# Joint 64-feature products for two pairs of weight blocks in the fourth batch's first MLP half

## The chip, the cores and the metric

The kernel runs on one core of one Trainium2 chip. Its engines work side by side, each on its own queue of instructions: TensorE (PE, matmuls, with PEld for the loads of its weights), VectorE (DVE), ScalarE (ACT), GpSimd (POOL) and SyncE (SP), which issues the transfers. They wait for each other through semaphores. Matmuls write to PSUM, which has eight banks of 512 float32 numbers in each of 128 partitions; the vector engines read it from there. The metric is the device time of one execution, in microseconds (us).

## The reference, cut to what matters

Two blocks follow each other, for 4 batches of 768 tokens. First an mLSTM cell with 8 heads of 40 features: a recurrence over the tokens with gates. Its output, 320 features per token, goes into a Fourier mixing block with an MLP:

```
X = np.real(np.fft.fft(np.fft.fft(x, axis=1), axis=2))
u = x + X
un = (u - mean(u)) / np.sqrt(var(u) + 1e-06)
out = u + np.maximum(un @ w_ch1, 0.0) @ w_ch2      # w_ch1: 320 x 1280, w_ch2: 1280 x 320
```

The change is in `un @ w_ch1`, the MLP's first half, of the last batch. All is in float32, and a float32 matmul runs in two passes, which the profile counts as two.

## The kernel before, in words

The program is written out by hand: `at(slot, phase, function, ...)` puts a call into a plan, and `run` carries the plan out in the order of slot and phase. So the order of each engine's queue follows from slots and phases alone; within a slot, phases run from EVAC (0) over FILL (1) and MAIN (2) to FILL_PE (3). Semaphores are put in by the language: an instruction waits for the earlier ones on other engines that use the same tile. Batches overlap: while one batch is in its MLP, the next is in its recurrence and its Fourier mix. The fourth batch has nothing behind it, so its MLP runs alone at the end.

The eight PSUM banks: four are handed out by number, as tiles `pm`, `po`, `px` and so on, by `bank(name, shape, n)`. The other four are two tiles of two banks each, `scores` and `heads` (named `ps` and `ph` in the profile), which serve the recurrence. When the fourth batch's MLP starts, the recurrence has ended and they are idle.

The first half for batches 1 to 3 (counted from 0): the 1280 hidden features are ten blocks of 128, taken as five pairs, numbered 0 to 4. The 768 tokens are two groups of 384, `gr` 0 and 1. The 320 input features are two parts of 128 (`ch` 0 and 1 of the weights, `mlp_u(gr, 0)` and `mlp_u(gr, 2)`) and one of 64 (`mlp_u(gr, 1)`). For each pair, the 2 x 2 block product over the two 128-feature parts is done with seven products in place of eight (Winograd's form), with sums of weights S2, S3, S4 and of inputs T2, T3, T4. The products go into four banks, which the code calls p1, p2, p5 and p3. What p1 holds is copied out by ScalarE in between, and the rest is added by VectorE. The 64 features that are left are multiplied in `rest_products` (line 1129): four matmuls on quarters of the array, 64 x 64 each, that run side by side, for each group of tokens.

`mlp_block(b, i, step)` (line 1207) issues pair i. Its steps, in order on TensorE:

- `begin(i)`: first product, into p1; ScalarE copies p1 to the hidden block `h11`, that is `hidden(0, 2i)`; its buffer is called h00 (h10, h11 and h01 are the buffers of `h12`, `h22` and `h21`). For pair 0 it runs at step 0, for the others at step 3 of the pair before.
- step 0: the product into p2.
- step 1: the S2 product on top of p1, which ScalarE copies to `h12`; the product into p5, which VectorE adds to `h12`.
- step 2: the S4 product into p3; the S3 product on top of p1, which ScalarE copies to `h22`.
- step 2.5: the 64-feature products, first of group 1 into p3 and p5, then of group 0 into p2 and p1. Then VectorE's three adds: p3 to `h12`, p5 to `h22`, p2 to `h11`.
- step 3: `begin(i + 1)`; then the T4 product on top of p1, from which ScalarE takes `h21` with a relu.

The three hidden blocks that VectorE finished get their relu in place by ScalarE in the next pair's slots (`mlp_relu_in_place`, planned at line 1391). An even pair takes its banks 3, 2, 1, 0 for p1, p2, p5, p3, an odd pair 0, 1, 2, 3. So `begin(i + 1)` writes into the bank that held p3 of pair i and waits for VectorE's add of it.

The second half (`mlp_out_pair`, line 1333) needs sums over hidden blocks, `hidden_sums` (line 1324), S1 to S4 in the profile. Those of the first pair of token tiles are planned at lines 1406 to 1409: for weight-block pairs 0 to 2 during the last slots of the first half, for pairs 3 and 4 at its end. `banks` in the lines quoted is, inside `mlp_block`, the list of bank numbers:

```
banks = list(range(4) if i % 2 else range(3, -1, -1))
```

Of the kernel before, what the change touches and what calls it, by code (L numbers as in the profile page):

```python
# [14 lines left out]
AF = mybir.ActivationFunctionType  # L15
# [3 lines left out]
B, H, S, D = 4, 8, 768, 40  # L19
L = 128  # L20
# [8 lines left out]
NFF = DFF // L  # L29
TAIL = DM - 2 * L  # L30
TG = NT // 2
# [26 lines left out]
def kernel(  # L58
# [15 lines left out]
    nc = tc.nc  # L74

    def pool(name, bufs, **kw):
        return ctx.enter_context(tc.tile_pool(name=name, bufs=bufs, **kw))
# [16 lines left out]
    def bank(name, shape, n=None):  # L94

        return ps_m.tile(shape, FP, name=name, tag=f"pm{next(turn) if n is None else n}")
# [31 lines left out]
    def at(slot, phase, fn, *args):  # L128
        plan.setdefault((slot, phase), []).append((fn, args))
# [7 lines left out]
    EVAC, FILL, MAIN, FILL_PE = range(4)  # L137
# [303 lines left out]
    class Piece:  # L441
# [15 lines left out]
        def take(self):  # L457
            if self.float:
                return
            n = self.src.shape[1]  # L460
            words = self.raw.bitcast(U32).rearrange("p (m two) -> p m two", two=2)
            self.lo, self.hi = words[:, :, 0], words[:, :, 1]
            self.e = cp.tile([L, n], U32, name="e", tag="e", bufs=1)
            self.m = cp.tile([L, n], U32, name="m", tag="m", bufs=1)
            nc.vector.tensor_scalar(out=self.e, in0=self.hi, scalar1=20, scalar2=0x7FF, op0=OP.logical_shift_right,  # L465
                                    op1=OP.bitwise_and)
            nc.vector.tensor_scalar(out=self.m, in0=self.hi, scalar1=0xFFFFF, scalar2=0x100000, op0=OP.bitwise_and,
                                    op1=OP.bitwise_or)
# [32 lines left out]
    def w1_block(ch, f):  # L501
        return w1_sb[:, f // 2, (2 * ch + f % 2) * L:(2 * ch + f % 2 + 1) * L]

    def w1_rest(n):
        return w1_sb[:, n, 4 * L:]
# [80 lines left out]
    def product(out, w, x, start):  # L586
        nc.tensor.matmul(out, w, x, start=start, stop=True, skip_group_check=True)  # L587
# [69 lines left out]
    banks = {}  # L657
# [10 lines left out]
    def half(n):  # L668
        return slice(n * LH, (n + 1) * LH)
# [459 lines left out]
    def rest_products(banks, n, u, start):  # L1129


        for cols in range(2):
            for i in range(2):
                nc.tensor.matmul(banks[i][half(cols)], w1_rest(n)[half(i), half(cols)], u[half(i)], start=start,  # L1134
                                 stop=not start, skip_group_check=True)
# [29 lines left out]
    def hidden(gr, f):  # L1165
        return hid[gr, f % 2][:, f // 2 * TG * L:(f // 2 + 1) * TG * L]
# [8 lines left out]
    def block(t, n):  # L1175
        return t[:, n * L:(n + 1) * L]
# [20 lines left out]
    def mlp_u(gr, ch):  # L1197
        return uT_bufs[gr][:, ch].rearrange("p c t -> p (c t)")
# [8 lines left out]
    def mlp_block(b, i, step):  # L1207

        k = mixes[b]
        f = 2 * i
        T2, T3, T4 = w1x["T"]
        A = {(r, ch): w1_block(ch, f + r) for r in range(2) for ch in range(2)}

        def product(bank, w, u, start=False):
            nc.tensor.matmul(bank, w, u, start=start, stop=True, skip_group_check=True)  # L1217

        def tails(gr, banks):
            rest_products(banks, i, mlp_u(gr, 1), False)  # L1220

        def add(h, bank):
            nc.vector.tensor_tensor(out=h, in0=h, in1=bank, op=OP.add)  # L1223

        banks = list(range(4) if i % 2 else range(3, -1, -1))

        def begin(i):


            k.p1 = bank("pm", [L, TG * L], 0 if i % 2 else 3)  # L1230
            product(k.p1, w1_block(0, 2 * i), mlp_u(0, 0), True)
            nc.scalar.copy(out=hidden(0, 2 * i), in_=k.p1)

        (h11, h21), (h12, h22) = ([hidden(gr, f + r) for r in range(2)] for gr in range(2))
        if step == 0:
            if i == 0:
                begin(0)
            k.pm = [k.p1, bank("pm", [L, TG * L], banks[1])]
            product(k.pm[1], A[0, 1], mlp_u(0, 2), True)
        elif step == 1:  # L1240
            k.pm.append(bank("pm", [L, TG * L], banks[2]))
            p1, _, p5 = k.pm
            if i == 0:
                product(p5, A[1, 0], mlp_u(1, 0), True)
            product(p1, block(w1x["S2"], i), T2)
            nc.scalar.copy(out=h12, in_=p1)
            if i > 0:
                product(p5, A[1, 0], mlp_u(1, 0), True)
            add(h12, p5)
        elif step == 2:  # L1250
            k.pm.append(bank("pm", [L, TG * L], banks[3]))
            p1, p2, p5, p3 = k.pm
            product(p3, block(w1x["S4"], i), mlp_u(1, 2), True)
            product(p1, block(w1x["S3"], i), T3)
            nc.scalar.copy(out=h22, in_=p1)
        elif step == 2.5:
            p1, p2, p5, p3 = k.pm
            tails(1, (p3, p5))
            tails(0, (p2, p1))
            add(h12, p3)  # L1260
            add(h22, p5)
            add(h11, p2)
        else:
            p1 = k.p1
            if i < NFF // 2 - 1:
                begin(i + 1)
            product(p1, A[1, 1], T4)
            nc.scalar.activation(out=h21, in_=p1, func=AF.Relu, scale=-1.0)

    def mlp_relu_in_place(gr, f):  # L1270
        h = hidden(gr, f)
# [109 lines left out]
    def plan_mlp(b, s):  # L1381
        groups = range(NT // TG)
        for i in range(NFF // 2) if b > 0 else ():
            for step in range(4):
                at(s, MAIN, mlp_block, b, i, step)
                if step == 2:
                    at(s, MAIN + 0.2, mlp_block, b, i, 2.5)
                s += 1
            end = i == NFF // 2 - 1
            for n, (gr, f) in enumerate(((1, 2 * i + 1), (1, 2 * i), (0, 2 * i))):  # L1390
                at(*((s - 1, MAIN + (-0.1 if gr else 0.1)) if end else (s + n, MAIN + 0.5)), mlp_relu_in_place, gr, f)
        for gr, n in IN_ORDER if b == 0 else ():
            for f in (2 * n, 2 * n + 1):
                at(s, MAIN, mlp_in, b, gr, f)
                s += 1
            i = IN_ORDER.index((gr, n))
            if i < 4 or i % 2 == 0 or i == 9:
                at(*((s, MAIN + 0.5) if i == 1 else (s, FILL_PE - 0.1) if i == 4 else
                     (s - 1, MAIN + (-0.1 if i in (2, 8, 9) else 0.2))), mlp_in_rests, b, i, False)
                if 3 < i < 8:  # L1400
                    at(*((s, FILL_PE - 0.05) if i == 4 else (s - 1, MAIN + 0.25)), mlp_in_rests, b, i + 1, i == 6)
            for f in (2 * n, 2 * n + 1):
                at(*((s - 1, MAIN + 0.3) if i == 0 else (s, FILL_PE + 0.2) if i == 4 else (s + (i == 1), EVAC)), mlp_relu,
                   b, gr, f)
        if b > 0:
            for j in range(1, 5):
                at(s - (5, 4, 3, 3)[j - 1], FILL_PE + 0.3, hidden_sums, 0, (j,), 0, NFF // 2 - 2)
            at(s, EVAC, hidden_sums, 0, (1, 2), NFF // 2 - 2, NFF // 2)
            at(s, MAIN + 0.1, hidden_sums, 0, (3, 4), NFF // 2 - 2, NFF // 2)
        for n in range(TG) if b > 0 else ():  # L1410
            for step in range(4):
                at(s, MAIN, mlp_out_pair, b, n, step)
                if n < TG - 1 and step > 1:
                    for j in (1, 2) if step == 2 else (3,) if b == 1 else (3, 4):
                        at(s, MAIN + 0.6, hidden_sums, n + 1, (j,))
                s += 1
        for gr in groups if b == 0 else ():
            for i in range(TG):
                for half in range(2):
                    at(s, MAIN, mlp_out, b, gr, i, half)  # L1420
                    s += 1
                n = gr * TG + i
                at(*((s + 2, MAIN + 0.1) if n == 0 else (s + 1, EVAC) if n == 1 else (s, EVAC)), mlp_store, b, gr, i)
# [76 lines left out]
    scores, heads = (pool(n, 1, space=PSUM).tile([L, 2, NP * L], FP, name=n) for n in ("ps", "ph"))  # L1500
# [146 lines left out]
```

## Time and profile before

| what | value |
|---|---|
| median of 3 runs (lowest to highest) | 381.68 us (380.98 to 381.75) |
| the profiled execution's own time | 382.09 us |
| its span from first to last instruction | 380.2 us |
| granted TensorE clock, mean | 0.999 |
| TensorE busy | 373.3 us, 98% |
| DVE, ACT, POOL busy | 280.8, 171.4, 133.9 us |
| fourth batch's first MLP half, from the first product to the last | 316.3 to 347.6 us |
| its 64-feature products (line 1134) start at | 320.4, 326.7, 332.9, 339.2, 345.4 us |

The profile gives each instruction's start and duration, and for an instruction before which its engine stood idle, what ended that time. Times are from the start of the span. A row of the timeline merges equal instructions that follow each other (x16). A matmul row says how large the part of the array is (128*128 or 64*64) and what goes out (128x384). Matmuls overlap: a product of two passes lasts 0.81 us, and the next can start before that is over. PEld rows stand for loads of weights, which usually run beside the matmul before.

### The profile page before, as it was taken

To read this page: it belongs to the slowest core of one execution; us is meant where nothing else is said; L and a number is where in the kernel's file an instruction comes from. 1 tells how busy PE (TensorE), PEld (TensorE's weight loads), DVE (VectorE), ACT (ScalarE), POOL (GpSimd) and SP (SyncE) were. 2 spreads that over 40 slices of the span, in tenths; PEclk is the share of its full clock that TensorE was granted. 3 is DMA by queue.
4 is the path that set the end of the run, shared out by engine and by line. 5 is a ranking of instruction groups with operands and counts; after the bars stand their busy time and mean duration, and the time that the engine had idled before them with its cause. 6 is when DMAs were issued, how large, how long until landed. Compare 5 with 4: busy or idle time off the path is not lost.

```text
span 380.2 us, 11433 instructions
## 1 busy us (share of the span) xinstructions
PE 373.3 (98%) x4602; PEld 278.2 (73%) x4602; DVE 280.8 (74%) x662; ACT 171.4 (45%) x501; POOL 133.9 (35%) x240
## 2 busy tenths in 40 slices
PE   8999999999999999999999999999999999999996
PEld 6887655567677777666578999676488996546996
DVE  7788999999998585787964787987745885245552
ACT  4878757756442114764442153854520233544000
POOL 5568433775686124471501424561300000020000
PEclk9999999999999999999999999999999999999999
DMA  7978565999870428460002737300000001000011
GB/s 195 284 219 287 168 184 148 252 241 265 278 207 29 127 66 238 134 174 26 0 3 62 205 99 195 102 3 3 0 2 34 17 20 36 0 0 2 34 36 34
DMA packets 20500, 41.93 MB, mean 110 GB/s; under 512 B 3256, under 2 KB 9744, under 8 KB 20320
## 3 DMA queue, kind: packets, MB, share of 16 engines
q1 hardware_dynamic: 20448, 41.21, 37.5%
q8 instruction: 36, 0.59, 0.7%
q14 instruction: 16, 0.13, 0.1%
HBM read 37.10 MB, written 4.10 MB: 108 GB/s over the span
## 4 chain that ended last, share of the span: by engine, by line
PE 79%; DVE 9%; ACT 2%; issue 1%; SPq 1%; POOL 1%; DMA 0%; DVEq 0%; ACTq 0%; POOLq 0%
PE po L1346 22%; PE pm L1217 19%; PE po L1289 8%; PE pm L1134 7%; PE ph L587 5%; PE pm L1151 4%; PE ps L587 4%; PE pu L1004 3%; PE pz L958 2%; PE put L1053 2%; PE pzt L958 1%; PE hb L587 1%; DVE e L480 1%; DVE stats L1027 1%; DVE e L465 1%
## 5 line engine op out<-in xcount | busy, mean ns | idle before, releaser
L1295 DVE SCALAR_TENSOR_TENSOR x<-po,rstd,x 128x160 f32<-128x160 f32 (+1 forms) x69 | 27.1, 394 | 36.3 <-PE po L1346 33.0
L1223 DVE TENSOR_TENSOR h<-h,pm 128x384 f32<-128x384 f32 x60 | 30.5, 550 | 24.2 <-PE pm L1217 11.8
L583 POOL TENSOR_SCALAR_AFFINE_SELECT W<-W 64x512 f32<-64x512 f32 x36 | 28.1, 780 | 37.8 <-ACT W L556 28.8
L1217 PE MATMUL pm<-uT,w_sb 128*128 128x384 f32 x90 | 37.3, 503 | 0.1
L556 ACT ACTIVATE W<-W,colT 128x64 f32<-128x64 f32 x144 | 36.6, 336 | 1.6 <-DMA W<-M_d 1.6
L710 POOL TENSOR_TENSOR C<-C,decB 128x164 f32<-128x164 f32 x33 | 18.1, 549 | 49.4 <-DVE C L717 45.9
L1289 PE MATMUL po<-w_sb,h 128*128 128x320 f32 x120 | 33.6, 432 | 0.0
L1134 PE MATMUL pm<-uT,w_sb 64*64 64x384 f32 x320 | 32.0, 496 | 0.0
L1077 POOL TENSOR_TENSOR t<-rstd 128x6 f32<-128x6 f32 x12 | 3.7, 311 | 76.1 <-DVE v L1071 75.6
L568 POOL TENSOR_TENSOR qg<-qk,Gb 128x512 f32<-128x512 f32 x21 | 28.1, 1337 | 4.5 <-DMA Gb<-G_d 4.2
L1289 PEld LDWEIGHTS po<-w_sb,h 128*128 128x128 f32 x120 | 22.5, 190 | 8.9
L1151 PE MATMUL pm<-uT,w_sb 128*128 128x384 f32 x80 | 28.4, 496 | 0.0
L1346 PE MATMUL po<-T,S 128*128 128x160 f32 x180 | 27.8, 301 | 0.2 <-DVE x L1295 0.2
L1346 PEld LDWEIGHTS po<-T,S 128*128 128x128 f32 x180 | 25.4, 190 | 1.3 <-DVE x L1295 0.4
L1346 PE MATMUL po<-w_sb,h 128*128 128x160 f32 x180 | 26.3, 300 | 0.0
L1346 PEld LDWEIGHTS po<-w_sb,h 128*128 128x128 f32 x180 | 25.2, 190 | 1.4 <-DVE x L1295 0.3
L1217 PEld LDWEIGHTS pm<-uT,w_sb 128*128 128x128 f32 x90 | 15.7, 189 | 12.1 <-DVE h L1223 4.1
L1272 ACT ACTIVATE h<-h 128x384 f32<-128x384 f32 x45 | 23.1, 520 | 2.9 <-DVE h L1223 2.9
L1134 PEld LDWEIGHTS pm<-uT,w_sb 64*64 64x64 f32 x320 | 11.1, 132 | 15.5 <-issue 13.4
L574 POOL TENSOR_TENSOR vw<-kvt,colT 128x328 f32<-128x328 f32 x23 | 19.6, 852 | 7.0 <-DVE colT L290 2.7
L1151 PEld LDWEIGHTS pm<-uT,w_sb 128*128 128x128 f32 x80 | 14.3, 190 | 10.1 <-issue 1.2
L587 PE MATMUL ps<-qk 40*64 40x64 f32 (+1 forms) x768 | 19.9, 240 | 0.3 <-DVE C L717 0.3
(255 smaller groups left out, 825.2 us busy)
## 6 DMA issues: line engine op xcount, KB each, us to landing
kvt<-in_kv SPq DMA_DIRECT2D x24, 336.0 KB
qk<-in_qkT SPq DMA_DIRECT2D x48, 160.0 KB
raw<-in_w SPq DMA_DIRECT2D x10, 640.0 KB
W<-M_d SPq DMA_DIRECT2D x36, 128.0 KB
so<-in_o SPq DMA_DIRECT2D x24, 160.0 KB
out<-x SPq DMA_DIRECT2D x23, 160.0 KB
Gb<-G_d SPq DMA_DIRECT2D x42, 80.0 KB
ds_sb<-in_dft_s SPq DMA_DIRECT2D x1, 1158.0 KB
```

Of the source, the lines that this page charges most:

```text
L556: nc.scalar.activation(out=k.W[:, h, :], in_=M, func=AF.Exp, scale=-1.0, bias=colT[:, c, 0, b * H + h:b * H + h + 1])
L568: nc.gpsimd.tensor_tensor(out=k.qg[:, :, t], in0=k.qk[:, 0, :, t], in1=k.Gb[:, :, t], op=OP.mult)
L583: nc.gpsimd.affine_select(out=W, in_=W, compare_op=OP.is_ge, fill=0.0, base=base, pattern=[[0, H], [-1 if back else 1, LH]], channel_multi ...
L587: nc.tensor.matmul(out, w, x, start=start, stop=True, skip_group_check=True)
L1134: nc.tensor.matmul(banks[i][half(cols)], w1_rest(n)[half(i), half(cols)], u[half(i)], start=start, stop=not start, skip_group_check=True)
L1151: nc.tensor.matmul(k.pm[i], w1_block(ch, f // 2 * 2 + i), u[2 * ch], start=(ch == 0 and not ahead), stop=(ch == 1 and (ahead or n in (2, 5 ...
L1217: nc.tensor.matmul(bank, w, u, start=start, stop=True, skip_group_check=True)
L1223: nc.vector.tensor_tensor(out=h, in0=h, in1=bank, op=OP.add)
L1272: nc.scalar.activation(out=h, in_=h, func=AF.Relu, scale=-1.0)
L1289: nc.tensor.matmul(k.po[m], hidden(gr, f)[:, i * L:(i + 1) * L], w2_sb[:, f, :], start=(f == 0), stop=(f == NFF - 1))
L1295: nc.vector.scalar_tensor_tensor(out=u, in0=po, scalar=k.rstd[:, c:c + 1], in1=u, op0=OP.mult, op1=OP.add)
L1346: nc.tensor.matmul(po, a[:, f], w[:, f], start=start and f == 0, stop=f == half - 1, skip_group_check=True)
```

## The change

In the last batch, the 64-feature products of pairs 0 and 1 are issued together, and those of pairs 2 and 3; pair 4 keeps its own. So that four more results can be held, the odd pairs 1 and 3 use the two banks of `scores` for p1 and p2 and the two of `heads` for p5 and p3. Even pairs use the four numbered banks, pair 2 in the other direction than pairs 0 and 4.

An even pair 0 or 2 issues nothing at step 2.5, and at step 3 only `begin` of the next pair. An odd pair issues at step 2.5 the 64-feature products of both pairs, group 1 first, and then six adds: both pairs' p3, both p5, both p2. At step 3 it issues the T4 products of both, and `begin(i + 1)` after them, where it stood ahead of T4. The relus in place of pairs 0 and 2 are planned four slots later, which sets them among those of pairs 1 and 3. The hidden sums of the last batch are split otherwise: pairs 0 and 1 early, pairs 2 and 3 in the last slot, pair 4 at the end. Batches 1 and 2 keep their order.

```diff
@@ mlp_block
         A = {(r, ch): w1_block(ch, f + r) for r in range(2) for ch in range(2)}
+        paired = b == B - 1
+        closes = {0: (), 1: (0, 1), 2: (), 3: (2, 3)}.get(i, (i,)) if paired else (i,)
+        if i == 0 and step == 0:
+            k.sets = {}
...
-        def tails(gr, banks):
-            rest_products(banks, i, mlp_u(gr, 1), False)
-
         def add(h, bank):
             nc.vector.tensor_tensor(out=h, in0=h, in1=bank, op=OP.add)
 
-        banks = list(range(4) if i % 2 else range(3, -1, -1))
+        def take(i):
+            n = len(k.sets.setdefault(i, []))
+            if paired and i % 2:
+                t = (banks["scores"], banks["heads"])[n // 2][:, n % 2, 0:TG * L]
+            else:
+                t = bank("pm", [L, TG * L], 3 - n if i % (4 if paired else 2) == 0 else n)
+            k.sets[i].append(t)
+            return t
 
         def begin(i):
-            k.p1 = bank("pm", [L, TG * L], 0 if i % 2 else 3)
-            product(k.p1, w1_block(0, 2 * i), mlp_u(0, 0), True)
-            nc.scalar.copy(out=hidden(0, 2 * i), in_=k.p1)
+            p1 = take(i)
+            product(p1, w1_block(0, 2 * i), mlp_u(0, 0), True)
+            nc.scalar.copy(out=hidden(0, 2 * i), in_=p1)
...
         elif step == 2.5:
-            p1, p2, p5, p3 = k.pm
-            tails(1, (p3, p5))
-            tails(0, (p2, p1))
-            add(h12, p3)
-            add(h22, p5)
-            add(h11, p2)
+            for gr in (1, 0):
+                for n in closes:
+                    p1, p2, p5, p3 = k.sets[n]
+                    rest_products((p3, p5) if gr else (p2, p1), n, mlp_u(gr, 1), False)
+            for h in range(3):
+                for n in closes:
+                    add(hidden(h < 2, 2 * n + h % 2), k.sets[n][(3, 2, 1)[h]])
         else:
-            p1 = k.p1
-            if i < NFF // 2 - 1:
+            if i < NFF // 2 - 1 and len(closes) < 2:
                 begin(i + 1)
-            product(p1, A[1, 1], T4)
-            nc.scalar.activation(out=h21, in_=p1, func=AF.Relu, scale=-1.0)
+            for n in closes:
+                p1 = k.sets[n][0]
+                product(p1, w1_block(1, 2 * n + 1), T4)
+                nc.scalar.activation(out=hidden(0, 2 * n + 1), in_=p1, func=AF.Relu, scale=-1.0)
+            if len(closes) > 1:
+                begin(i + 1)
@@ plan_mlp
-                at(*((s - 1, MAIN + (-0.1 if gr else 0.1)) if end else (s + n, MAIN + 0.5)), mlp_relu_in_place, gr, f)
+                late = 4 * (b == B - 1 and i % 2 == 0)
+                at(*((s - 1, MAIN + (-0.1 if gr else 0.1)) if end else (s + late + n, MAIN + 0.5)), mlp_relu_in_place, gr, f)
...
+            last = NFF // 2 - (1 if b == B - 1 else 2)
             for j in range(1, 5):
-                at(s - (5, 4, 3, 3)[j - 1], FILL_PE + 0.3, hidden_sums, 0, (j,), 0, NFF // 2 - 2)
-            at(s, EVAC, hidden_sums, 0, (1, 2), NFF // 2 - 2, NFF // 2)
-            at(s, MAIN + 0.1, hidden_sums, 0, (3, 4), NFF // 2 - 2, NFF // 2)
+                if b == B - 1:
+                    at(s - 1, FILL + 0.3, hidden_sums, 0, (j,), 2, last)
+                at(s - (5, 4, 3, 3)[j - 1], FILL_PE + 0.3, hidden_sums, 0, (j,), 0, 2 if b == B - 1 else last)
+            at(s, EVAC, hidden_sums, 0, (1, 2), last, NFF // 2)
+            at(s, MAIN + 0.1, hidden_sums, 0, (3, 4), last, NFF // 2)
```

More of the change, by code (lines that the diff above doesn't have):

```diff
@@ L1214, in mlp_block @@
         A = {(r, ch): w1_block(ch, f + r) for r in range(2) for ch in range(2)}
+        paired = b == B - 1
+        closes = {0: (), 1: (0, 1), 2: (), 3: (2, 3)}.get(i, (i,)) if paired else (i,)
+        if i == 0 and step == 0:
+            k.sets = {}
         def product(bank, w, u, start=False):
             nc.tensor.matmul(bank, w, u, start=start, stop=True, skip_group_check=True)
-        def tails(gr, banks):
-            rest_products(banks, i, mlp_u(gr, 1), False)
         def add(h, bank):
             nc.vector.tensor_tensor(out=h, in0=h, in1=bank, op=OP.add)
-        banks = list(range(4) if i % 2 else range(3, -1, -1))
+        def take(i):
[6 more added lines that the diff above has]
+            return t
         def begin(i):
-            k.p1 = bank("pm", [L, TG * L], 0 if i % 2 else 3)
-            product(k.p1, w1_block(0, 2 * i), mlp_u(0, 0), True)
-            nc.scalar.copy(out=hidden(0, 2 * i), in_=k.p1)
-        (h11, h21), (h12, h22) = ([hidden(gr, f + r) for r in range(2)] for gr in range(2))
+            p1 = take(i)
+            product(p1, w1_block(0, 2 * i), mlp_u(0, 0), True)
+            nc.scalar.copy(out=hidden(0, 2 * i), in_=p1)
+        h12, h22 = (hidden(1, f + r) for r in range(2))
         if step == 0:
@@ L1237, in mlp_block @@
                 begin(0)
-            k.pm = [k.p1, bank("pm", [L, TG * L], banks[1])]
-            product(k.pm[1], A[0, 1], mlp_u(0, 2), True)
+            product(take(i), A[0, 1], mlp_u(0, 2), True)
         elif step == 1:
-            k.pm.append(bank("pm", [L, TG * L], banks[2]))
-            p1, _, p5 = k.pm
+            p5 = take(i)
+            p1 = k.sets[i][0]
             if i == 0:
@@ L1250, in mlp_block @@
         elif step == 2:
-            k.pm.append(bank("pm", [L, TG * L], banks[3]))
-            p1, p2, p5, p3 = k.pm
+            p3 = take(i)
+            p1 = k.sets[i][0]
             product(p3, block(w1x["S4"], i), mlp_u(1, 2), True)
@@ L1256, in mlp_block @@
         elif step == 2.5:
-            p1, p2, p5, p3 = k.pm
-            tails(1, (p3, p5))
-            tails(0, (p2, p1))
-            add(h12, p3)
-            add(h22, p5)
-            add(h11, p2)
-        else:
-            p1 = k.p1
-            if i < NFF // 2 - 1:
+            for gr in (1, 0):
[5 more added lines that the diff above has]
+                    add(hidden(h < 2, 2 * n + h % 2), k.sets[n][(3, 2, 1)[h]])
+        else:
+            if i < NFF // 2 - 1 and len(closes) < 2:
                 begin(i + 1)
-            product(p1, A[1, 1], T4)
-            nc.scalar.activation(out=h21, in_=p1, func=AF.Relu, scale=-1.0)
+            for n in closes:
[4 more added lines that the diff above has]
+                begin(i + 1)
     def mlp_relu_in_place(gr, f):
```

## The prediction

> **What bounds the kernel now.** I read the page's busy shares and chain first, then the table of stages, then the waits and the timeline of the stage that the change touches. All times are microseconds unless marked.
>
> ```profile
> span 380.2 us, 11433 instructions
> PE 373.3 (98%) x4602; PEld 278.2 (73%) x4602; DVE 280.8 (74%) x662; ACT 171.4 (45%) x501; POOL 133.9 (35%) x240
> PE 79%; DVE 9%; ACT 2%; issue 1%; SPq 1%; POOL 1%; DMA 0%; DVEq 0%; ACTq 0%; POOLq 0%
> ```
>
> TensorE is busy 98% of the span and holds 79% of the chain of work that ended last. The stages, with the columns PE, weight loads, DVE, ACT, POOL busy, granted clock, DMA share and GB/s:
>
> ```profile
> 0.00:20.00 20.00, 18.35 (x190) 14.99 (x192) 14.17 (x32) 13.25 (x45) 11.86 (x37) 1.00 0.80 236
> ...
> 316.10:320.40 4.30, 4.30 (x15) 2.18 (x13) 2.66 (x6) 0.96 (x2) 0.00 (x0) 1.00 0.13 45
> 320.40:345.40 25.00, 24.94 (x121) 12.53 (x120) 10.22 (x24) 12.31 (x27) 2.50 (x12) 1.00 0.00 1
> 345.40:350.40 5.00, 5.00 (x40) 3.69 (x39) 3.03 (x7) 2.63 (x6) 0.00 (x0) 1.00 0.01 3
> ```
>
> From 316.3 to 347.6 lies the fourth batch's first MLP half: five weight-block pairs, 0 to 4. In it TensorE is never free (24.94 of 25.00), while DVE and ACT are half idle. So a gap put on TensorE here is a gap in the span. The waits of 316 to 350 that hold TensorE are three, and small (total, times, longest):
>
> ```profile
> PEld pm L1134 <- issue: 3.6, 10, 0.5
> PEld pm L1217 <- DVE h L1223: 2.7, 4, 0.7
> PEld pm L1217 <- ACT h L1246: 0.5, 1, 0.5
> ```
>
> They stand on weight loads, which usually run beside the matmul before, so only a part is lost. What is lost shows in the starts (timeline; start, duration, engine, line, operation):
>
> ```profile
> 318.21 0.81 PE L1217 MATMUL pm<-raw 128*128 128x384 f32 x2
> 318.85 0.81 PE L1217 MATMUL pm<-uT,raw 128*128 128x384 f32 x2
> 319.05 0.48 ACT L1246 COPY h<-pm 128x384 f32<-128x384 f32 x1 [1.46 <-PE pm L1217]
> 319.58 0.30 PEld L1217 LDWEIGHTS pm<-e,raw 128*128 128x128 f32 x2 [0.54 <-ACT h L1246]
> ...
> 324.65 0.81 PE L1217 MATMUL pm<-uT,w_sb 128*128 128x384 f32 x2
> 325.29 0.81 PE L1217 MATMUL pm<-uT,raw 128*128 128x384 f32 x2
> 325.56 0.55 DVE L1223 TENSOR_TENSOR h<-h,pm 128x384 f32<-128x384 f32 x1 [2.73 <-PE pm L1217]
> 325.94 0.81 PE L1217 MATMUL pm<-e,raw 128*128 128x384 f32 x2
> 326.68 1.52 PE L1134 MATMUL pm<-uT,w_sb 64*64 64x384 f32 x16
> 327.60 1.49 DVE L1223 TENSOR_TENSOR h<-h,pm 128x384 f32<-128x384 f32 x3 [1.49 <-PE pm L1134]
> 328.21 0.91 PE L1217 MATMUL pm<-uT,w_sb 128*128 128x384 f32 x2
> 328.96 0.81 PE L1217 MATMUL pm<-m,w_sb 128*128 128x384 f32 x2
> 346.87 0.30 PEld L1217 LDWEIGHTS pm<-m,w_sb 128*128 128x128 f32 x2 [0.60 <-issue]
> 347.40 0.94 ACT L1272 ACTIVATE h<-h 128x384 f32<-128x384 f32 x2 [0.97 <-DVE h L1223]
> ```
>
> From these rows come all my prices.
> - A product (two passes) starts 0.645 after the one before (324.65, 325.29, 325.94). After TensorE stood waiting, the second product starts 0.75 later (328.21 to 328.96): a restart costs 0.105, the weight load that wasn't made ahead.
> - Product to ScalarE's copy of its bank: 0.84 (318.21 to 319.05). Copy to a TensorE instruction that waits for it: 0.53 (319.05 to 319.58). Together 1.37.
> - Product to VectorE's add of its bank: 0.91 (324.65 to 325.56). Add to a TensorE instruction that waits for it: 0.61 (327.60 to 328.21, the first of three adds). Together 1.52. Adds in a row start every 0.467 ((1.49 less 0.55) / 2).
> - A visit of one pair to the 64-feature form: entry 0.74 for 0.645 (325.94 to 326.68), 1.53 (326.68 to 328.21) for the 1.29 that four groups of four at 0.3225 need, and the restart, 0.105. That is 0.095 + 0.24 + 0.105 = 0.44 lost. The last pair, whose next product waits for no add, takes 1.45 (its sixteen start at 345.42, the next product at 346.87), so 0.36 is the form's own price and 0.08 the wait for VectorE. Five visits stand 6.245 apart.
>
> **The change, part by part.** All before the first product of pair 1 keeps its order, and so do POOL's and SP's queues throughout; batches 1 and 2 are the same.
>
> *Removed.* Pairs 0 and 1 share one visit, pairs 2 and 3 another; pair 4 keeps its own. Four visits at 0.44 become two at 0.36, since the product behind a joint visit (T4 of the even pair) has nothing to wait for: 1.76 less 0.72 is a gain of 1.04. Bounds: 0.72 (two at 0.36) to 1.3 if the joint visits also hid their entry.
>
> *Added: four kinds of wait.* An odd pair's four results lie in two tiles of two banks: `scores` holds p1 and p2, `heads` p5 and p3. The changed kernel's order has waits there that the old one has not, because the order is kept tile by tile, not bank by bank:
>
> ```
> 1038 L1221 Matmult ps<-uT_103,w_sb 128x384
> 1039 L1221 Matmult ps<-uT_103,w_sb 128x384 [waits Activation_49]
> 1041 L1221 Matmult ph<-uT_104,w_sb 128x384
> 1042 L1221 Matmult ph<-uT_104,raw 128x384 [waits DVE_49]
> 1050 L1221 Matmult ps<-m,w_sb 128x384 [waits DVE_49]
> ```
>
> 1. *p2 of an odd pair* waits until ScalarE has copied p1 from the other half of `scores`. Before, T4 of the last pair stood between the two; now p2 is next. Pair 1: 1.37 for 0.645 is 0.725, and the restart: 0.83. Behind it stand all of the pair's products. Pair 3 is worse, since the relus of pairs 0 and 1 moved four slots later, and two of them (of h00) now stand in ScalarE's queue between the copy from pair 2's S3 product and that of p1: from S3's start 0.84, then 0.38 (copy to relu, 326.78 to 327.16), 0.43 (relu to relu, 0.94 less 0.51) and again 0.43 to the copy, 0.53 to TensorE, 2.61 in all. The order would need 1.29, so 1.32 and 0.105: 1.43. Bounds 0.83 (relus free) to 1.75 (no overlap on ScalarE, 0.53 each).
> 2. *The S4 product into p3* waits for VectorE's add of p5 from the other half of `heads`: 1.52 for 0.645 is 0.875, and the restart, 0.98; twice, 1.96. Bounds 0.8 to 1.1 each, by the spread of the rows.
> 3. *T4 of an odd pair* into p1 waits for the last of the six adds behind the joint visit, that of p2. From the visit's start: first add after 0.92 (326.68 to 327.60), the second needs the second group pair, 0.645 later, then four more at 0.467, and 0.61: 4.04. T4 of the even pair starts at 1.45 + 1.29 = 2.74 and the odd one could at 3.49. So 0.55 and a restart, 0.655; twice, 1.31. Bounds 0.655 to 1.0 (adds unpipelined, 0.56 each).
> 4. *S2 of pairs 2 and 4* waits for the copy of p1, as before; T4 no longer stands between, so two products cover 1.29 of 1.37: 0.08 and a restart, 0.185; twice, 0.37. Bounds 0 to 0.4.
>
> Sum: 0.83 + 1.43 + 1.96 + 1.31 + 0.37 = 5.90 added, 1.04 removed, **4.86 slower**.
>
> *Moved, at no cost.* The first half of the hidden sums is split in 0-2, 2-4 and 4-5. The four pieces for pairs 2 and 3 (128x256, 0.42 each) now stand behind pair 4's adds; VectorE idles 1.33 there, waiting for ScalarE's last relu, and the two pieces behind that wait shrink to 128 columns. If the cover is too short, the first residual moves by 0.1. ScalarE's twelve moved relus read finished sums; only pair 3's copy stands behind them, counted above. Between the waits ScalarE (12.31 of 25) and VectorE (10.22) have room.
>
> *Against the median.* The profiled execution took 382.09 (span 380.2 and 1.9 around it), 0.41 above the median of the runs, 381.68. 382.09 + 4.86 is 386.95 for such an execution; for the median 381.68 + 4.86 = **386.5**.
>
> **Two rules of the Trainium skill.** The tile-wide waits are no demand of the banks: the Trainium skill, PSUM — Partial Sum Buffer, section on bank collisions, asks that PSUM be guarded by bank and quadrant; p1 and p2 are in different banks. If only that held, waits 1, 2 and 3 would vanish: the first rival. The other speaks against the change: TensorE: Matmul & The Clock Gate, Part 1 in the Trainium skill, halves TensorE's clock after an idle window of about 3.4 us, and its section on HAM oscillation tells of micro-idles that did so. The table shows 1.00 even in the first 20, with 1.65 idle; by the window my gaps of 1.4 at most would cost nothing, but by the second section repeated ones might: the second rival.
>
> **The rivals.**
> - *The tile-wide waits are met in time* (the other side). It would need each copy and add on the neighbouring bank to end before TensorE arrives, within 0.645 instead of 1.37 and 1.52. Then only 0.37 is added: 381.68 − 1.04 + 0.37 = 381.0, faster by 0.18%; without the S2 waits 380.6, faster by 0.28%. It decides when a copy returns in half its present time; every row speaks against it, as ACT and DVE start only when the product has ended. 5% (same 3%, faster 2%).
> - *The granted clock falls in the stretch.* TensorE would idle some 5 in 35, in pieces. If one joint visit then ran at half the clock, its eight groups of 0.3225 would take 2.58 more: 389.1. It decides once a clock under 1.00 is granted; that it was 1.00 in every stage before 350, the first 20 included, speaks against. 4%.
> - *ScalarE and VectorE don't overlap their queues behind the joint visit* (0.53 per relu, 0.56 per add): 0.32 + 0.7 more, 387.5. 9%. The rows of three adds in 1.49 speak against.
> - *Only part of the waits bind*, by the low bounds (pair 3's copy ahead of the relus' cost, adds earlier): 0.6 for the first and 0.4 for the second less, 385.5. 7%.
>
> **How the numbers follow.** The forecast, all four waits as priced, holds 75%: 386.5, by itself 386.0 to 387.0. The range takes in the low and high cost bounds, 385.4 to 387.9, and leaves out the first rival and most of the clock. Slower by over 0.2% (0.76, about what a measurement of this kernel can tell from no change): 0.75 + 0.04 + 0.09 + 0.07 = 0.95; same 0.03; faster 0.02.
>
> **What would show it.** In the changed profile: one 64-feature row of x32 in about 2.7 at two places; ScalarE's copy from `ps` directly ahead of a weight load of `ps` that stood idle (near 1.2 in pair 1, 1.8 in pair 3); a load of `ph` released by DVE; T4 into `ps` released by DVE 1.3 behind T4 into `pm`; pair 4's 64-feature row near 350.3 instead of 345.42, and the rest of the program as before. I am wrong if these loads show no idle time ended by ACT or DVE, if the clock leaves 1.00, or if the stage after 350 changes length.

## The result, and the profile after

| | kernel before | changed kernel |
|---|---|---|
| median (lowest to highest), 6 runs each | 381.33 us (380.68 to 382.28) | 384.14 us (383.61 to 389.16) |
| ratio, with its 95% interval | | 1.0119 (1.0079 to 1.0158) |
| the same once more on another occasion, 33 and 10 runs | 381.25 us | 385.05 us; 1.011 (1.0072 to 1.0148) |
| profiled execution, span | 380.2 us | 381.7 us |

The change makes the kernel slower: the ratio gives 1.2%, about 4.5 us, as forecast (386.5 for 381.68 is a ratio of 1.0127). The medians by themselves stand 2.81 apart, and 3.80 on the second occasion, and the median of the six runs, 384.14, lies under the range that was given. Single runs of one kernel differ by several us: four of the six lie near 383.9 and two near 388.8. For the profiled execution (383.63) the trace shows where it gained. Pair 0's S4 product starts at 315.69, 3.16 earlier than in the kernel before, although the program is the same up to there. So its span is only 1.5 us longer. The stretch that the change touches is not disturbed by this, and there the comparison is exact. Ratios, their intervals and the means below leave out runs over 1.5% above the fastest of the same kernel.

The page of the changed kernel, the lines that answer to those shown before:

```profile
span 381.7 us, 11432 instructions
PE 371.3 (97%) x4602; PEld 275.3 (72%) x4602; DVE 279.5 (73%) x666; ACT 171.2 (45%) x501; POOL 132.2 (35%) x240
PE 85%; DVE 8%; issue 1%; ACT 1%; DVEq 0%; ACTq 0%
```

The stages of the changed kernel, cut at pair 0's S4 product and at pair 4's 64-feature products (the columns are those of the prediction's table):

```profile
315.70:347.10 31.40, 27.47 (x125) 12.55 (x123) 10.50 (x25) 12.26 (x27) 2.50 (x12) 1.00 0.02 6
347.10:381.70 34.60, 31.54 (x229) 29.59 (x228) 17.68 (x41) 3.04 (x7) 0.00 (x0) 1.00 0.08 29
```

In the kernel before, the same stretch ran from 318.85 to 345.42, which is 26.57; here it is 31.43 (315.69 to 347.12). That is 4.86 more, to the hundredth what the price list gave. TensorE, never free there before, now stands for 3.9 of 31.4. That is less than 4.86 because busy rows hide a part of each wait: a row lasts 0.81 or 0.91, though the next product can start after 0.645. The granted clock stayed at 1.00. The stage behind it shrank from 34.75 (345.42 to the end, 380.17) to 34.59.

What holds TensorE now, from the waits of 316 to 350 in the changed kernel (total, times, longest):

```profile
PEld ps L1221 <- ACT h L1240: 2.9, 2, 1.7
PEld ph L1221 <- DVE h L1224: 2.7, 2, 1.3
PEld pm L1134 <- issue: 2.5, 8, 0.5
PEld ps L1221 <- DVE h L1224: 2.0, 2, 1.0
PEld pm L1221 <- ACT h L1240: 1.1, 2, 0.5
```

The first, second, fourth and fifth are the forecast's waits 1, 2, 3 and 4, each twice. The wait on `pm` for VectorE's add, 2.7 in the kernel before, is gone. The timeline shows each in its place: the loads of weights in front of which TensorE stood, and the products that they are measured from.

```profile
317.17 0.81 PE L1221 MATMUL ps<-uT,w_sb 128*128 128x384 f32 x2
318.02 0.48 ACT L1240 COPY h<-ps 128x384 f32<-128x384 f32 x1 [0.17 <-PE ps L1221]
318.55 0.30 PEld L1221 LDWEIGHTS ps<-uT,w_sb 128*128 128x128 f32 x2 [1.18 <-ACT h L1240]
...
319.94 0.81 PE L1221 MATMUL ph<-uT,w_sb 128*128 128x384 f32 x2
320.86 0.56 DVE L1224 TENSOR_TENSOR h<-h,ph 128x384 f32<-128x384 f32 x1 [3.90 <-PE ph L1221]
321.47 0.30 PEld L1221 LDWEIGHTS ph<-uT,raw 128*128 128x128 f32 x2 [1.33 <-DVE h L1224]
...
322.96 0.88 PE L1134 MATMUL pm<-uT,w_sb 64*64 64x384 f32 x8
325.70 0.91 PE L1221 MATMUL pm<-m,w_sb 128*128 128x384 f32 x2
326.41 0.55 DVE L1224 TENSOR_TENSOR h<-h,ps 128x384 f32<-128x384 f32 x1
327.01 0.30 PEld L1221 LDWEIGHTS ps<-m,w_sb 128*128 128x128 f32 x2 [1.02 <-DVE h L1224]
...
331.18 0.81 PE L1221 MATMUL pm<-e,raw 128*128 128x384 f32 x2
332.02 0.48 ACT L1262 COPY h<-pm 128x384 f32<-128x384 f32 x1 [0.62 <-PE pm L1221]
332.40 0.94 ACT L1283 ACTIVATE h<-h 128x384 f32<-128x384 f32 x2
333.23 0.47 ACT L1240 COPY h<-ps 128x384 f32<-128x384 f32 x1
333.75 0.30 PEld L1221 LDWEIGHTS ps<-uT,w_sb 128*128 128x128 f32 x2 [1.74 <-ACT h L1240]
```

Top to bottom: p2 of pair 1 starts 1.38 behind p1, once p1's bank next door has been copied. S4 starts 1.53 behind p5, once p5's bank next door has been added. After the joint visit's start (322.96) the even T4 comes at 2.74 and the odd one at 4.05, released by the sixth add. And in pair 3, two relus stand between ScalarE's copies, so that p2 starts 2.57 behind pair 2's S3.

### The profile page after: what moved, and what is told of

The parts are those of the page before. It is cut to its first block, busy times and chain, and to the rows that moved or that the text cites. A ratio compares the mean times of both kernels' runs of the same rounds, so it can differ in the third digit from the quotient of the medians.

```text
span 381.7 us, 11432 instructions
## 1 busy us (share of the span) xinstructions
PE 371.3 (97%) x4602; PEld 275.3 (72%) x4602; DVE 279.5 (73%) x666; ACT 171.2 (45%) x501; POOL 132.2 (35%) x240
## 4 chain that ended last, share of the span: by engine, by line
PE 85%; DVE 8%; issue 1%; ACT 1%; DVEq 0%; ACTq 0%
PE po L1357 22%; PE pm L1221 16%; PE po L1300 8%; PE pm L1134 6%; PE ph L587 5%; PE ps L587 5%; PE pm L1151 4%; PE pu L1004 3%; PE pz L958 2%; PE hb L587 2%; PE ps L1221 2%; PE put L1053 2%; DVE h L1224 2%; PE pzt L958 1%; PE pz L970 1%
## 5 line engine op out<-in xcount | busy, mean ns | idle before, releaser
L1224 DVE TENSOR_TENSOR h<-h,pm 128x384 f32<-128x384 f32 x52 | 26.8, 550 | 21.3 <-PE pm L1134 10.7
L1221 PE MATMUL pm<-uT,w_sb 128*128 128x384 f32 x78 | 31.7, 501 | 0.0
L1134 PE MATMUL pm<-uT,w_sb 64*64 64x384 f32 x288 | 29.3, 496 | 0.0
L1151 PE MATMUL pm<-uT,w_sb 128*128 128x384 f32 x80 | 28.4, 496 | 0.0
L1151 PEld LDWEIGHTS pm<-uT,w_sb 128*128 128x128 f32 x80 | 14.3, 190 | 10.1 <-issue 1.2
L1221 PEld LDWEIGHTS pm<-uT,w_sb 128*128 128x128 f32 x78 | 13.7, 189 | 8.9 <-DVE h L1224 1.4
L1134 PEld LDWEIGHTS pm<-uT,w_sb 64*64 64x64 f32 x288 | 9.9, 132 | 13.9 <-issue 12.3
```

What stands on the lines that cost most here:

```text
L1151: nc.tensor.matmul(k.pm[i], w1_block(ch, f // 2 * 2 + i), u[2 * ch], start=(ch == 0 and not ahead), stop=(ch == 1 and (ahead or n in (2, 5 ...
```

## Experiments

The theory: TensorE waits because an odd pair's results share a tile, and each wait costs what the rows gave. Its rivals: the two recurrence tiles are slow in themselves, or joint visits save nothing. All stretches run from pair 0's S4 product to pair 4's 64-feature products; 26.57 before, 31.43 changed. Four of the kernels below ran once: the other pairing (383.73), the relus behind the copy (384.58), the next first product between the two T4 (386.82) and an odd pair's first product ahead of S3 (385.09), with the kernel before at 383.28 beside them. One run says little of whole times here, so only their stretch is used.

**The two kernels once more.** No edit.

> The changed kernel unchanged. The four waits' theory: from the start of pair 0's S4 product to pair 4's 64-feature products 31.4 us again (26.6 in the kernel before). For the rest of the time: if TensorE's clock at the start of a run is a matter of the run, times fall in groups some 3 to 5 us apart, and the eight first 128x128 matmuls last 1.1 us in the fast group and 2.0 in the slow one. If the changed kernel itself starts faster, they last 1.1 in all its runs and 2.0 in all runs of the kernel before.

> The kernel before unchanged. Clock a matter of the run: some of its runs are 2.6 to 3.2 us faster than the median so far, near 378.5, and its eight first matmuls last 1.1 or 2.0 us. The kernel's own doing: all its runs near 381.3 and 2.0 us.

The stretch: 31.44 and 26.57. Of the twelve further runs of the kernel before, four were under 380, the lowest 379.32. The ten of the changed kernel, 383.16 to 388.63, show no two clear groups. The first eight 128x128 matmuls of the program, in the first profiled executions of the kernel before and of the changed one:

```profile
4.97 2.04 PE L233 MATMUL pM<-Mq,ident 128*128 128x128 f32 x8
```

```profile
4.97 1.13 PE L233 MATMUL pM<-Mq,ident 128*128 128x128 f32 x8
```

They start in the same hundredth and last 2.04 or 1.13. In the second execution of the kernel before they last 1.40, and in a variant of the changed kernel below (the other pairing) 2.05, so the start is a matter of the run, not of the change. The clock column of the stages reads 1.00 there all the same: the trace's first clock record stands at 10.83 us in the first of the two executions and at 4.76 in the second, and ahead of a first record the column prints 1.00. One part of the expectation missed: the second profiled execution of the changed kernel is among the slowest (388.51), yet its eight matmuls last 1.13. Its loss lies elsewhere, as the last section shows.

**Four tiles in place of two.** The odd pairs' results in four tiles of one bank each, in the same four banks, the order unchanged.

```diff
-                t = (banks["scores"], banks["heads"])[n // 2][:, n % 2, 0:TG * L]
+                t = banks["apart"][n]
...
+    run(s_mlp + 3 * MLP_SLOTS)
+    ps_late.close()
+    pq = pool("pq", 1, space=PSUM)
+    banks.update(apart=[pq.tile([L, TG * L], FP, name=f"pq{n}", tag=f"pq{n}") for n in range(4)])
```

> As the changed kernel, but an odd pair's four results lie in four tiles of one bank each. The theory of the tile-wide waits: waits 1, 2 and 3 vanish, what is left is 0.185 at S2 of pairs 1, 2 and 4 and 0.78 at S2 of pair 3 (two relus ahead of the copy of p1), 1.34 in all against a gain of 1.04, so 26.9 from pair 0's S4 to pair 4's 64-feature products, 0.3 more than before and 4.6 less than the changed kernel. If the banks of the recurrence themselves were slow to read or write, it stays near 31.4.

Measured: 26.84 for 26.9 expected; 381.6 us, a ratio of 1.0008 (0.9973 to 1.0043). The waits of that stretch:

```profile
PEld pq L1221 <- ACT h L1240: 1.6, 2, 1.1
PEld pm L1221 <- ACT h L1240: 1.1, 2, 0.5
PEld pm L1221 <- ACT h L1253: 0.5, 1, 0.5
```

No load waits for VectorE, and those that wait for ScalarE wait for a copy of their own bank. The tile's border, not the bank, made waits 1 to 3.

**The same two tiles, paired otherwise.** p1 and p3 in `scores`, p2 and p5 in `heads`.

```diff
-                t = (banks["scores"], banks["heads"])[n // 2][:, n % 2, 0:TG * L]
+                t = banks["heads" if n in (1, 2) else "scores"][:, n // 2, 0:TG * L]
```

> As the changed kernel, with the same two tiles, but p1 and p3 of an odd pair lie in one and p2 and p5 in the other. If only the tile shared with a bank still being read makes TensorE wait, waits 1 and 3 vanish; S4 then waits for the copy of p1 behind S2, 0.185 instead of 0.98; S2 waits 0.185 in pairs 1, 2 and 4 and 0.78 in pair 3. Sum 0.185 x 5 + 0.78 = 1.7 against 1.04: 27.24 in the stretch. If the two recurrence tiles are slow in themselves, near 31.4.

Measured: 27.53, 0.29 over what was expected, and 3.90 under the changed kernel by one line. The miss is at T4 (timeline of this kernel):

```profile
325.70 0.88 PE L1134 MATMUL pm<-uT,w_sb 64*64 64x384 f32 x8
328.63 0.56 DVE L1224 TENSOR_TENSOR h<-h,ps 128x384 f32<-128x384 f32 x1 [1.45 <-PE ps L1134]
329.24 0.30 PEld L1221 LDWEIGHTS ps<-m,w_sb 128*128 128x128 f32 x2 [0.51 <-DVE h L1224]
```

I had T4 free, since the add of p3 could start 1.565 into the visit. It starts after 2.93: the add reads `scores`, and so waits for the last 64-feature products into `scores`, those of p1. Waits by tile bind in both directions. T4 came 0.05 late and lost a restart, 0.15, twice.

**Relus behind the copy.** The relus of h00 of pairs 0 and 1 one slot later, behind the copy of pair 3's p1.

```diff
                 late = 4 * (b == B - 1 and i % 2 == 0)
+                late += b == B - 1 and i < 2 and n == 2
```

> As the changed kernel, but the relus in place of h00 of pairs 0 and 1 stand behind the copy of pair 3's p1 in ScalarE's queue. From pair 0's S4 to pair 4's 64-feature products: 31.43 less 0.6 (pair 3's p2 then waits 1.37 like pair 1's, not 1.97), 30.83. If ScalarE's relus were not what made pair 3's wait longer, 31.43.

Measured: 30.88, 0.55 less; pair 3's p2 now waits as pair 1's does (1.18 in the load's row in place of 1.74):

```profile
334.77 0.30 PEld L1221 LDWEIGHTS ps<-uT,w_sb 128*128 128x128 f32 x2 [1.18 <-ACT h L1240]
```

**The next first product between the two T4.**

```diff
             for n in closes:
+                if n == i and len(closes) > 1:
+                    begin(i + 1)
                 p1 = k.sets[n][0]
...
-            if len(closes) > 1:
-                begin(i + 1)
```

> As the changed kernel, but the next even pair's first product stands between the two T4 products. It fills the wait of T4 for the sixth add (0.655) and puts two products between p1 and S2 of pairs 2 and 4 (0.185): 1.68 less over both joint visits, 29.75. If T4's wait is for something later than the sixth add, it moves less than 1.

Measured: 29.76. T4's load stands idle 0.37 in place of 1.02, with a useful product in the gap, and S2 of pairs 2 and 4 no longer waits.

**An odd pair's first product ahead of S3.** After the S4 product of an even pair.

```diff
             product(p3, block(w1x["S4"], i), mlp_u(1, 2), True)
+            if paired and not closes:
+                begin(i + 1)
             product(p1, block(w1x["S3"], i), T3)
...
-            if i < NFF // 2 - 1 and len(closes) < 2:
+            if i < NFF // 2 - 1 and len(closes) == 1:
                 begin(i + 1)
```

> As the changed kernel, but an odd pair's first product stands ahead of S3 of the pair before, and its copy ahead of the relus. p2 of pair 1 waits 0.185 instead of 0.83, that of pair 3 0.185 instead of 1.43, and S3 of pair 0 no longer loses 0.19: 2.08 less, 29.35. If the waits of p2 are not for the copy of p1, 31.4.

Measured: 29.39. This order alone takes back 2.04, though the tiles are the changed kernel's (0.19 of it is the wait at pair 0's S3, which the kernel before has too).

**Four tiles and both orders.** The three edits (four tiles, between, ahead) together.

> As four_tiles, and the first product of an odd pair stands ahead of S3 of the pair before, that of the next even pair between the two T4 products. By the price list no TensorE wait of a copy is left before pair 4: 26.57 less 1.04 less the 0.185 that S3 of pair 0 lost, 25.35. The whole 1.2 us below the kernel before, 0.3%. If the form's price is not saved by joint visits, 26.4.

> The version with four tiles and the new order once more, beside the kernel before. Its stretch was 25.32 us against 26.57, and the second half behind it 0.16 shorter, so 1.4 us of 381 or 0.37% is expected, a ratio of 0.9963. If the stretch's gain came back elsewhere, 1.0.

Measured: a stretch of 25.32 both times, 1.25 below the kernel before, and 34.59 and 34.60 behind it. The second execution around the first joint visit:

```profile
322.71 0.81 PE L1221 MATMUL pq<-e,raw 128*128 128x384 f32 x2
323.45 0.88 PE L1134 MATMUL pm<-uT,w_sb 64*64 64x384 f32 x8
...
325.43 0.83 PE L1134 MATMUL pq<-uT,w_sb 64*64 64x384 f32 x8
326.19 0.91 PE L1221 MATMUL pm<-m,w_sb 128*128 128x384 f32 x2
326.94 0.81 PE L1221 MATMUL pm<-uT,w_sb 128*128 128x384 f32 x2
327.58 0.81 PE L1221 MATMUL pq<-m,w_sb 128*128 128x384 f32 x2
```

No instruction of ACT or DVE holds TensorE in it; all that is left is the form's own price. Whole runs: 380.86 us, ratio 0.9977 (0.9948 to 1.0007), and 380.25 us, 0.9975 (0.9945 to 1.0005). Each interval just takes in 1, so neither alone shows a gain. On the first occasion the mean is 0.70 under that of the kernel before (11 and 43 runs), on the second 1.05 (11 and 23), together 0.88 with a standard error of 0.34 (from the spreads of the sets), or 0.23%. With every run counted it is 0.52 with 0.45. So whole runs make a gain likely and do not settle its size; the trace has 1.4 us, 0.37%.

**One more idle product at the start**, on that version.

```diff
-        idle_products(3, rest)
+        idle_products(4, rest)
```

> The same with four idle products at the program's start instead of three. If the scatter of some 3 us between runs is TensorE's clock, which is granted in full at 4.2 to 6.5 us in some runs and at 10.8 in others because TensorE isn't busy long enough without a break, one more product of 1 us makes the late starts rarer: fewer runs over 382, at a cost of up to 1 us where the first transposes come later. If the start doesn't depend on it, the times are those of the other version, or up to 1 us more.

Measured: 380.75 us, 0.9998 (0.9975 to 1.0021) of the kernel before, stretch 25.32. Two runs of twelve were over 382, against one of twelve for the version without it beside it, and the lowest times were no lower. The expectation of fewer runs over 382 was not met. Whether late rises of the clock grew rarer can't be told from these runs, and the times gained nothing.

## Why the prediction was right

- *The bound.* TensorE was the bound of the stretch, and the gaps put there came out in it: 4.86. Right. That the sum was met to the hundredth is partly luck, since deviations of up to 0.04 in its terms cancel.
- *Wait 1.* 1.38 for 1.37 in pair 1, 2.57 for 2.61 in pair 3; moving the relus took 0.55 of the 0.6 that was put down to them. The prediction calls the relus of pairs 0 and 1 moved, twelve in all; the diff moves six, those of pairs 0 and 2. The two that stand ahead of the copy are as it said.
- *Wait 2.* 1.53 for 1.52, both times.
- *Wait 3.* 4.05 and 4.06 for 4.04.
- *Wait 4.* 1.38 and 1.37 for 1.37.
- *The gain.* Joint visits end at 2.74, as worked out. With all waits gone the stretch is 1.25 shorter, against 1.04 and the 0.185 of pair 0's S3.
- *Hidden sums.* Costed at nothing; the second half is 0.16 shorter, since the two pieces behind the last relu shrank from 256 to 128 columns. The first residual add behind them comes 4.38 after pair 4's 64-feature products began, in place of 4.54. The sum should have had −0.16: 4.70, for the 4.5 or so of whole runs. A change of length of the stage after 350 was one of the prediction's own signs of being wrong; it came, by 0.16.
- *The rival of waits met in time* is refuted: with two tiles they were not met, with four they weren't there. The Trainium skill, PSUM — Partial Sum Buffer, section on bank collisions, asks for a guard by bank and quadrant, of which by bank is the simple form. Four tiles of one bank each guard by bank; their stretch, 26.84, is the one worked out from the rows with waits 1 to 3 gone (26.9).
- *The rivals of the bounds* did not come true: two relus took 0.94, the adds behind a joint visit followed each other every 0.47, and all four waits bound at their prices.
- *The rival of the clock.* It stayed at 1.00 throughout the stretch with gaps up to 1.1 between matmuls. (The micro-idles that the prediction cites from the Trainium skill, TensorE: Matmul & The Clock Gate, stand there in the section on psum-queue depth-cycling, not in that on HAM oscillation.) But one ground that I gave was wrong: I read the 1.00 of the first 20 us as a full clock, while eight matmuls there took 2.04 in place of 1.13.
- *The scale.* I set the forecast on a median of three runs as if single runs agreed within some tenths. Runs of the kernel before spread from 378.55 to 385.98, so the median of the six missed the range though the ratio did not, and most intervals of the ratios reach 0.3 to 0.4% to each side, where the prediction counted on 0.2%. The range was also narrower than its bounds: all low ones together make 385.0, all high ones 388.1.

## What to carry to other kernels

Where a framework orders by tile, a tile should not be larger than what is produced and read as one: two banks in one tile made each read of one bank block the writes to the other, which in this order cost 4.59 (31.43 against 26.84), some four times what the joint visits can save. A chain of product, copy and product again took 1.37 here, a little over two product times; the order has to put two other products between. And a change of a few us is read in its own stretch of the trace, from one fixed instruction to another, not in whole runs that differ by more.

## What the runs showed of the hardware

TensorE's clock at the start differs from run to run. The same eight matmuls took between 1.13 and 2.05 in the profiled executions: 2.04 and 1.40 in two of the kernel before, 1.13 in both of the changed kernel, 1.87 with four tiles. In the two executions compared in the result, the same matmul near 11 us starts at 11.12 and 8.45, 2.67 apart. But that is only a part of the scatter. Three profiled executions whose eight matmuls took 1.13, and whose clock did not fall ahead of the stretch, reach pair 0's S4 product at 315.69 (changed kernel), 317.26 (relus behind the copy) and 319.19 (first product ahead of S3), and the program is the same up to there.

The clock can fall in the middle, too. In the second profiled execution of the changed kernel (386.6), the stages around 87 us:

```profile
83.00:86.80 3.80, 1.65 (x115) 1.53 (x107) 2.91 (x5) 0.98 (x4) 1.47 (x3) 1.00 0.92 281
86.80:90.20 3.40, 3.40 (x15) 1.98 (x8) 2.80 (x8) 1.50 (x6) 1.65 (x3) 0.50 0.95 208
```

After 3.8 us in which TensorE was busy for 1.65, with transfers at 92%, it got half its clock for 3.4 us. The gap ahead of the same matmuls, in this execution, in that of the kernel with the next first product between the two T4, and in the second of four tiles and both orders:

```profile
86.46 0.63 PE L587 MATMUL ph<-kvt,W 64*64 64x41 f32 x18 [2.15 <-issue]
```

```profile
86.07 0.54 PE L587 MATMUL ph<-kvt,W 64*64 64x41 f32 x18 [1.60 <-issue]
```

```profile
86.69 0.54 PE L587 MATMUL ph<-kvt,W 64*64 64x41 f32 x18 [1.49 <-issue]
```

Behind 2.15 and 1.60 the clock fell to half for 3.4 us, and behind 3.35 (the first execution of four tiles and both orders) for 6.8. Behind 1.49, and behind 1.42 (relus behind the copy), it did not, nor behind the 1.1 of the stretch. These are six executions and no experiment: how busy TensorE was around the gap may count as well as its length. Whether the runs near 388.8 had such a stretch can't be seen without their traces; they share with this one a mean granted clock of 0.996. The Trainium skill, TensorE: Matmul & The Clock Gate, Part 1, has the half clock after an idle window of about 3.4 us; here gaps of 1.60 and 2.15 were enough. What share of busy time keeps the clock stays open.
